# Two-bank projection tiles, wide evictions on fixed engines and a rearranged first and last step in a dilated neighbourhood-attention kernel

## The chip, the cores and the metric

The kernel runs on one core of one Trainium2 chip. The metric is device time in microseconds (us), the median of several executions; executions of one kernel mostly agree within 0.3%. Profiles are single executions and come out some 1 to 3 us shorter than the timed median, because a span runs from the first to the last instruction. The granted clock in the profiles is the share of full speed that the throttle allowed PE; it is 1.00 in the stretch of the middle shown for each kernel below, but not everywhere in the start.

Engine names in the profile: PE is the matrix engine (PEld its weight loads), DVE is VectorE, ACT is ScalarE, POOL is GpSimd, SP is SyncE, which here only issues transfers. A "q" after a name (SPq, ACTq) is that engine's sequencer, for instance issuing a transfer.

## The reference

Attention over a 7 x 7 neighbourhood with dilation 2 on a 224 x 224 image with 192 channels, one head, bfloat16.

```python
def reference(x, wqkv, wo):                       # x (1,224,224,192), wqkv (192,576), wo (192,192)
    qkv = x @ wqkv                                # q, k, v: thirds of the last axis
    r0 = clip(arange(H) - 6, 0, H - 1 - 12)       # first row and column of each window,
    c0 = clip(arange(W) - 6, 0, W - 1 - 12)       # clipped at the edges of the image
    nidx = ...                                    # 49 neighbours: r0 + 0,2..12 by c0 + 0,2..12
    logits = einsum('bnc,bnkc->bnk', q, k[nidx]) * C ** -0.5
    p = softmax(logits)
    o = einsum('bnk,bnkc->bnc', p, v[nidx]) @ wo
```

## The kernel before

Two folds make the matrix work small. Scores use `x A x` with A = Wq Wk^T times the scale (tiles `aw`), so "queries" are x times A (tiles `ga`, `gb`) and "keys" are plain copies of x in another order (`xa`, `xb`; `xb` also holds one-hot rows which meet mask rows in `gb`, so that a matmul adds the mask). The value side uses WP = Wv Wo, so `vw` = x WP is already projected; its column C is one, so the product `y` of exponentials and `vw` holds the softmax sum beside the sum itself.

The work is 28 **steps** (a row parity `rc` and a block of 16 rows `j`), each of seven **ticks**. A tick forms the scores in PSUM (`s`), takes the exponential on ScalarE (`p_sb`), multiplies it with `vw` into PSUM (`y`, one buffer), takes the reciprocal of the sum (`rs`) and writes the scaled result (`o_sb`) on VectorE, and stores it. Between ticks stand the projections of the next step: `pv` products evicted into `vw`, `pg` products evicted into the queries, `pe` products of the edge columns evicted into `ge`. The first tick of every step also makes one `oe` (48 x 192), so **`oe` on VectorE marks a step** in every trace below. The program order on each engine is the order in which the code emits.

```python
ps_go = tc.tile_pool(name="ps_go", bufs=4, space=PSUM)      # one-bank tiles for pv, pg, pe
...
def evac(out, in_, n):                                      # ScalarE or VectorE, by a running estimate
    ca, cd = 60 + 0.95 * n, 70 + 1.15 * n
    if load["A"] + ca <= load["D"] + cd: load["A"] += ca; nc.scalar.copy(out=out, in_=in_)
    else:                                load["D"] += cd; nc.vector.tensor_copy(out=out, in_=in_)
...
def make_keys(k, rc):                                       # GpSimd, reading at a step of two rows, 448 bytes
    nc.gpsimd.tensor_copy(out=oa[:, rc, cc].rearrange("p n (c r) -> p (n c) r", r=BR),
                          in_=t[:, 2 * cc, rc::2, :].rearrange("p r j -> p j r"))
...
def vw_item(k, rc, i):                                      # two key blocks: half a tile per evac
    pv = ps_go.tile([128, 2, 256], F32, name="pv", tag="go")
    ...
    for cc in range(2):
        evac(VW[h:h + 64, rc, cc, 2 * i:2 * i + 2, 0:C], pv[h:h + 64, :, 0:C], 2 * C)
...
def store(dst, src): nc.sync.dma_start(out=dst, in_=src)    # every store on SyncE
...
for ti, i in enumerate(range(NQ - 1, -1, -1)):
    T = s_stage(rc, j, i)            # scores and exponential
    ...                              # this tick's vw items
    if pend: v_stage(pend); out_stage(pend)
    ...                              # this tick's query items
    pend = T
```

The softmax here doesn't subtract the row's maximum and nothing guards it: scores larger than these inputs give would overflow.

## Time and profile before

| | us |
|---|---|
| time, median of 3 (range) | 457.87 (457.26 to 459.14) |
| `oe` of step 2 (two steps done) | 74.21 |
| `oe` of the last step, 25 steps later | 391.59 |
| span | 455.9 |

So the span divides into a start of 74.2 us, a middle of 317.4 us (12.70 us a step) and an end of 64.3 us. These are the marks, from VectorE's timeline (start, duration, engine, line, operation, out<-in with shapes, count; in brackets the idle time before it and what ended it):

```profile
74.21 0.35 DVE L436 TENSOR_TENSOR oe<-y,rse 48x192 bf16<-48x192 f32 x1
...
391.59 0.35 DVE L436 TENSOR_TENSOR oe<-y,rse 48x192 bf16<-48x192 f32 x1
```

The middle, as a stretch from 110 to 136 us: its length, then busy time (and instructions) of PE, PEld, DVE, ACT and POOL, the granted clock, the DMA share and GB/s. PE and VectorE are at 81%, nothing is full.

```profile
110.00:136.00 26.00, 21.04 (x529) 18.71 (x525) 21.10 (x53) 18.84 (x41) 16.60 (x25) 1.00 0.49 112
```

Groups of instructions (line, engine, operation, shapes, count; busy us, mean ns of one; idle time before them and what ended most of it). Both engines empty halves of `pv` in small pieces; ScalarE waits 36.8 us in all for VectorE's half of the same tile, and PE's `y` waits for the outputs (54.3 us):

```profile
L231 DVE CAST vw<-pv 64x384 bf16<-64x384 f32 x237 | 130.6, 554 | 45.3 <-PE pv L259 26.4
L411 PE MATMUL y<-vw,p_sb 128*64 128x193 bf16 (+1 forms) x1540 | 102.6, 248 | 59.8 <-DVE o_sb L452 54.3
...
L228 ACT CAST vw<-pv 64x384 bf16<-64x384 f32 x169 | 79.5, 472 | 42.2 <-DVE vw L231 36.8
```

The end, from SyncE's timeline: the last output is formed at 401 us, and from 405.2 on SyncE issues 72 stores in 48.75 us, 0.68 us each.

```profile
385.67 7.58 SPq L416 DMA_DIRECT2D out_dram<-o_sb  x7
393.35 11.75 SPq L416 DMA_DIRECT2D out_dram<-oe  x16
405.20 48.75 SPq L416 DMA_DIRECT2D out_dram<-o_sb  x72
```

### The profile page before, as it was taken

Reading aid. Unit: us, or ns where it says so; the run is one execution under the profiler, and the core shown is the slowest. Engines: PE = TensorE matmul, PEld = TensorE weight load, DVE = VectorE, ACT = ScalarE, POOL = GpSimd, SP = SyncE. Lnnn points to the kernel's source line nnn. Section 1 sums busy time; section 2 is a strip of 40 time slices with the busy share of each in tenths; the row PEclk is TensorE's granted clock in tenths of the full one; section 3 lists DMA queues with packets and bytes.
Section 4 is the critical chain, followed back from the end, with each engine's and each line's share of the span. In section 5 each row is a group of like instructions: output and inputs, shape, how many; then the busy total and the mean of one; then the engine's idle time right before and its main releaser. Section 6 shows DMA issues by size and latency. Waiting matters only on the chain.

```text
span 455.9 us, 17843 instructions
## 1 busy us (share of the span) xinstructions
PE 311.7 (68%) x7448; PEld 272.8 (60%) x7448; DVE 313.4 (69%) x764; ACT 281.8 (62%) x592; POOL 244.2 (54%) x393
## 2 busy tenths in 40 slices
PE   4734588788887988797878988787878887600000
PEld 2434478787777877786767877777767777500000
DVE  6586688887887877887787877887788887610000
ACT  6423677787777777787777777787776877400000
POOL 8999981776749292947658193857658200000000
PEclk9977999999999999999999999999999999955555
DMA  9316536364362636373472838273452222100000
GB/s 204 85 23 142 133 121 152 91 140 107 76 145 73 150 85 155 78 140 94 97 139 56 149 78 163 71 151 91 96 135 62 64 54 63 36 9 20 20 8 4
DMA packets 108607, 42.85 MB, mean 94 GB/s; under 512 B 83204, under 2 KB 108270, under 8 KB 108526
## 3 DMA queue, kind: packets, MB, share of 16 engines
q1 hardware_dynamic: 108078, 41.42, 40.4%
q8 instruction: 58, 0.95, 1.0%
q10 hardware_dynamic: 448, 0.30, 0.3%
q14 instruction: 23, 0.19, 0.1%
HBM read 0.29 MB, written 19.35 MB: 43 GB/s over the span
## 4 chain that ended last, share of the span: by engine, by line
DVE 31%; PE 28%; ACT 11%; issue 8%; DMA 5%; POOL 4%; SPq 1%; DVEq 0%; ACTq 0%; POOLq 0%
DVE vw L231 12%; DVE o_sb L452 11%; PE y L411 10%; PE pg L321 6%; PE pv L259 5%; DMA out_dram<-o_sb 5%; ACT vw L228 4%; DVE rs L450 4%; PE s_88 L392 3%; ACT p_sb L395 3%; PE s_87 L392 2%; PE pe L279 1%; ACT ga_100 L228 1%; ACT gb_104 L228 1%; POOL xb_93 L240 1%
## 5 line engine op out<-in xcount | busy, mean ns | idle before, releaser
L231 DVE CAST vw<-pv 64x384 bf16<-64x384 f32 x237 | 130.6, 554 | 45.3 <-PE pv L259 26.4
L411 PE MATMUL y<-vw,p_sb 128*64 128x193 bf16 (+1 forms) x1540 | 102.6, 248 | 59.8 <-DVE o_sb L452 54.3
L411 PEld LDWEIGHTS <-p_sb 128*64 128x64 bf16 (+1 forms) x1540 | 78.3, 106 | 78.9 <-issue 75.8
L452 DVE TENSOR_TENSOR o_sb<-y,rs 128x384 bf16<-128x384 f32 x196 | 109.3, 558 | 7.0 <-DVE rs L450 0.3
L228 ACT CAST vw<-pv 64x384 bf16<-64x384 f32 x169 | 79.5, 472 | 42.2 <-DVE vw L231 36.8
L321 PEld LDWEIGHTS <-aw 128*64 128x64 bf16 x1008 | 61.8, 112 | 2.2 <-issue 1.1
L395 ACT ACTIVATE p_sb<-s_87 128x448 bf16<-128x448 f32 x98 | 53.5, 546 | 10.5 <-PE s_87 L392 9.3
L395 ACT ACTIVATE p_sb<-s_88 128x448 bf16<-128x448 f32 x98 | 53.5, 546 | 8.0 <-PE s_88 L392 6.2
L392 PEld LDWEIGHTS <-xa_90 128*64 128x64 bf16 x532 | 48.8, 111 | 2.2 <-issue 0.6
L392 PEld LDWEIGHTS <-xa_91 128*64 128x64 bf16 x532 | 49.1, 110 | 1.5
L392 PEld LDWEIGHTS <-xb_93 128*64 128x64 bf16 x420 | 36.8, 112 | 19.9 <-issue 16.4
L392 PEld LDWEIGHTS <-xa_92 128*64 128x64 bf16 x448 | 41.1, 110 | 1.3
L450 DVE RECIPROCAL rs<-y 128x2 f32<-128x2 f32 x196 | 32.2, 164 | 13.6 <-PE y L411 11.0
L228 ACT CAST ga_100<-pg 128x436 bf16<-128x436 f32 x55 | 28.5, 521 | 19.2 <-PE pg L321 18.7
L228 ACT CAST ga_101<-pg 128x436 bf16<-128x436 f32 x51 | 26.5, 522 | 19.7 <-PE pg L321 19.5
L392 PEld LDWEIGHTS <-xb_94 128*64 128x64 bf16 x420 | 37.3, 111 | 1.0
L259 PE MATMUL pv<-WP,xa_90 128*64 128x192 bf16 x280 | 32.1, 254 | 0.8 <-POOL xa_90 L238 0.6
L392 PEld LDWEIGHTS <-xb_95 128*64 128x64 bf16 x336 | 28.8, 111 | 3.3 <-DVE gb_104 L231 1.2
L392 PEld LDWEIGHTS <-xb_96 128*64 128x64 bf16 x336 | 29.5, 111 | 2.1 <-issue 1.0
L259 PE MATMUL pv<-WP,xa_91 128*64 128x192 bf16 x280 | 30.7, 246 | 0.0
L259 PE MATMUL pv<-WP,xb_93 128*64 128x192 bf16 x224 | 25.7, 255 | 1.5 <-POOL xb_93 L240 1.5
L259 PE MATMUL pv<-WP,xa_92 128*64 128x192 bf16 x224 | 24.8, 246 | 0.0
(226 smaller groups left out, 1068.9 us busy)
## 6 DMA issues: line engine op xcount, KB each, us to landing
out_dram<-o_sb SPq DMA_DIRECT2D x162, 96.0 KB
out_dram<-o_sb SPq DMA_DIRECT2D x27, 60.0 KB
out_dram<-oe SPq DMA_DIRECT2D x54, 9.0 KB
out_dram<-o_sb SPq DMA_DIRECT2D x54, 12.0 KB
out_dram<-o_sb SPq DMA_DIRECT2D x54, 9.0 KB
xb_95<-xb_93 SPq DMA_DIRECT2D x4, 112.0 KB
xb_96<-xb_94 SPq DMA_DIRECT2D x4, 112.0 KB
xe_97<-xa_90 SPq DMA_DIRECT2D x1, 448.0 KB
```

The source lines that it names most:

```text
L228: nc.scalar.copy(out=out, in_=in_)
L231: nc.vector.tensor_copy(out=out, in_=in_)
L240: nc.gpsimd.tensor_copy(out=ob[ps, rc, cc].rearrange("p n (c r) -> p (n c) r", r=BR), in_=t[ps, 1, rc::2, :].rearrange("p r j -> p j r"))
L259: nc.tensor.matmul(pv[h:h + 64, m, 0:C], lhsT=keys(k, rc, cc)[kt][:, 2 * i + m, :], rhs=WP[:, cc, kt, :], start=(kt == 0), stop=(kt == 1))
L279: nc.tensor.matmul(pg[64 * h:64 * h + 64, g], lhsT=AW[w][:, 64 * h:64 * h + 64], rhs=r, start=(i == 0), stop=(i == 1))
L321: nc.tensor.matmul(pg[64 * h:64 * h + 64, a_ - ra:b_ - ra, :], lhsT=AW[w][:, 64 * h:64 * h + 64], rhs=xt[b][:, k, l, :], start=(i == 0), s ...
L392: nc.tensor.matmul(o[h:h + 64, :, rs], lhsT=keys(k, rc, cc)[kt][:, n, :], rhs=mv[:, cc, CW * n:CW * n + QW, rs], start=(kt == 0), stop=(kt ...
L395: nc.scalar.activation(out=T.p[:].rearrange("p a b -> p (a b)"), in_=ps[:, 0:4 * QW * BR], func=ACTF.Exp)
L411: nc.tensor.matmul(o, lhsT=l, rhs=rhs, start=st, stop=True, skip_group_check=True)
L450: nc.vector.reciprocal(out=rs[:], in_=y_bank[:, :, sl, C:C + 1])
L452: nc.vector.tensor_tensor(out=o[:], in0=y_bank[:, :, sl, 0:C], in1=rs[:].to_broadcast([128, 2, C]), op=ALU.mult)
```

## The change

The intent: fewer and wider evictions, less work for GpSimd, an earlier start and an end that isn't a queue of store issues.

- Projection tiles take two PSUM banks (two slots instead of four). A `pv` tile holds four key blocks; VectorE evicts one half of the partitions in one 64 x 768 copy, ScalarE the other. Queries are evicted by ScalarE in 128 x 848 copies; the high half goes to a staging tile `hs` that GpSimd splits.
- Keys are copied in an order that GpSimd can read at unit stride.
- In a tick, `y` and the output come ahead of the projections.
- Outputs of two tiles at the end of a step are scaled in one instruction; small stores go to GpSimd's queue. In the last step outputs are gathered in `oall` and stored by few transfers on three queues.
- At the start, masks and one-hots are partly spread by transfers, the first keys are shared by VectorE and GpSimd, and work that the first scores don't need is deferred into steps 0 and 1.

```diff
-    ps_go = ctx.enter_context(tc.tile_pool(name="ps_go", bufs=4, space=PSUM))
+    ps_go = ctx.enter_context(tc.tile_pool(name="ps_go", bufs=2, space=PSUM))
 ...
+    mask_cols(4, nc.vector.tensor_copy); mask_rows(4, 0, nc.vector.tensor_copy)
 ...
+    for k in range(2):
+        nc.vector.memset(s_bank[k][:], NEG)
     for cc in range(2):
         h = 64 * ((1 + cc) % 2)
-        nc.gpsimd.memset(VW[h:h + 64, 0, cc, :, 0:C], 0.0)
+        nc.vector.memset(VW[h:h + 64, 0, cc], 0.0)
 ...
-            nc.gpsimd.tensor_copy(out=oa[:, rc, cc].rearrange("p n (c r) -> p (n c) r", r=BR),
-                                  in_=t[:, 2 * cc, rc::2, :].rearrange("p r j -> p j r"))
+        eng(out=dst.rearrange("p n (r c) -> p r n c", c=CW),
+            in_=t[ps, 2 * cc if kt == 0 else 1, rc::2, :].rearrange("p r (n c) -> p r n c", c=CW))
 ...
-            pv = ps_go.tile([128, 2, 256], F32, name="pv", tag="go")
+            pv = ps_go.tile([128, 2, 2, 256], F32, name="pv", tag="go")
-            for cc in range(2):
-                evac(VW[h:h + 64, rc, cc, 2 * i:2 * i + 2, 0:C], pv[h:h + 64, :, 0:C], 2 * C)
+            for cc, eng in ((0, nc.vector.tensor_copy), (1, nc.scalar.copy)):
+                eng(out=VW[h:h + 64, rc, cc, n0:n1, 0:C], in_=pv[h:h + 64]...[:, 0:n1 - n0, 0:C])
 ...
+            if kind < 2:
+                put(nc.scalar.copy, A[:, kind], slice(0, 128))
+            elif direct: ...
+            else:
+                hs = work.tile([128, SQ, BR], BF, name="hs", tag="hs", bufs=2)
+                put(nc.scalar.copy, hs[:], slice(0, 128))
+                for cc in range(2): nc.gpsimd.tensor_copy(out=Bt[ps, cc, 6:S, ra:rb], in_=hs[ps, 6:S, ra:rb])
 ...
+    last_qs = [nc.sync, nc.gpsimd, nc.scalar]
+        def pick(q):
+            if not last: return q
+            qn[0] += 1
+            return last_qs[qn[0] % 3]
 ...
-            for _ in range(-(-len(v_q) // left)): v_q.pop(0)()
             if pend:
                 v_stage(pend)
                 out_stage(pend)
+            for _ in range((len(v_q) > (NQ - ti) // 2) + (len(v_q) > NQ - ti)): v_q.pop(0)()
```

## The prediction

> **What bounds it now.** Three stages with different limits. (1) Start: by the timeline the second score tick runs at 39.8 us; VectorE builds masks from 25.6 to 37.6 us in front of evacuations, and GpSimd copies eight key tiles (1.70 us each) before the edge columns. (2) Middle: the `oe` instruction, one per step, goes from 62.3 to 379.9 us in 25 steps, 12.7 us each. By busy time over 110 to 136 us PE has 81%, VectorE 81%, ScalarE 72%, GpSimd 64%: none is full; the chain of waits (DVE 31%, PE 28%) runs y, reciprocal, `o_sb`, y with `vw` evacuations between. (3) End: the last `o_sb` is done at 401 us, the span is 455.9. Store issues fill it: 72 `o_sb` stores from 405.2 take SP 48.75 us, 0.68 us each.
>
> **What changes, costed.**
> - End: after the last output about 24 stores remain, 8 on each of three queues: 6 us at 0.7 us, 2 us landing, more on GpSimd: about 9 us. Saves 45 us.
> - Start: masks by DMA, first keys shared by VectorE and GpSimd, all else later. First score tick at 18-19 us; but steps 0 and 1 take deferred work, so 14 and 16 us. `oe` of step 2 at about 50 us, now 74.2: saves about 23 us.
> - Middle, per step: 14 `vw` halves (0.554 us VectorE, 0.472 ScalarE) become 4 + 4; a 64x768 one should take 0.95 and 0.79 us (slopes from narrower ones). Eight query evacuations become three of 128x848, 0.88 us. VectorE falls to 8.9 us, ScalarE stays at 9.3, PE about 10.2 (twice the edge matmuls). GpSimd's key copies get unit-stride reads; the Trainium skill, GPSIMD Engine Reference, Performance pitfalls for Q7 kernels, puts reads at steps over 8 bytes about 50% dearer; here the 224-byte-step copy takes 1.72 us, one as long with a small step 0.92. So 4 x about 1 us plus two `hs` copies and two DMA issues, under 10 us.
>
> **Why I do not book the busy time saved.** In the changed program's order ScalarE's `vw` evacuation waits for VectorE's of the same tile (serialized now too: 36.8 us of "ACT vw <- DVE vw"), and the next exponential stands behind it. The chain over two ticks, `o_sb`, vw on VectorE 0.95, vw on ScalarE 0.79, exp 0.55, y 0.53, reciprocal and o 0.77, is about 3.5 us; three pairs and the single tick with its double output give 12.4 to 13 us a step. Wider evacuations lengthen this latency while the sum shrinks. So the middle stays near 12.7 us.
>
> **Sum.** 50 + 25 x 12.7 + 11 (last step) + 9 = 388, plus 2 us between span and time: **390 us**, range **368 to 405**. Faster by over 2%: 0.98; within: 0.015; slower: 0.005.
>
> **What would show it.** Right: last `o_sb` to end of span under 12 us; `oe` of step 2 near 50 us; 12.2 to 13.2 us per step; "ACT vw <- DVE vw" among the longest waits; key copies near 1 us; PE still about 80% busy in the middle. Wrong: a step of 11 us or less, set by PE, would mean the vw chain overlaps better (about 345 us in all); key copies still 1.7 us with GpSimd over 90% busy would mean 13 us or more from GpSimd; a tail over 15 us would mean stores on GpSimd or ScalarE cost more than 0.7 us.

(The "224-byte-step copy" is a slip: the code reads every second row of 112 bfloat16 values, a step of 224 elements or 448 bytes.)

## The result, and the profile after

The changed kernel takes **418.7 us** (418.11 to 418.88). Ratios here are the mean time of one kernel's fast runs over that of the other's of the same rounds, so not quite the ratio of the medians quoted: 0.9137, interval 0.9103 to 0.9171. It is faster by 8.6%, and 28.7 us slower than predicted; the predicted range (368 to 405) does not hold it.

The same marks as above divide the span of 417.1 us:

```profile
74.18 0.35 DVE L462 TENSOR_TENSOR oe<-y,rse 48x192 bf16<-48x192 f32 x1
...
393.54 0.35 DVE L462 TENSOR_TENSOR oe<-y,rse 48x192 bf16<-48x192 f32 x1
```

| part | before | predicted | after |
|---|---|---|---|
| start, to `oe` of step 2 | 74.21 | 50 | 74.18 |
| middle, per step | 12.70 | 12.7 | 12.77 |
| end, from the last `oe` | 64.3 | 20 | 23.6 |

All of the gain comes from the end (40.7 us); the middle gives 2 us back, and the start gives nothing.

**The middle.** In the same stretch of 26 us VectorE fell from 21.1 to 17.7 us of work and ScalarE from 18.8 to 17.5, and the step did not shorten:

```profile
110.00:136.00 26.00, 22.48 (x563) 20.48 (x559) 17.71 (x39) 17.46 (x30) 16.05 (x32) 1.00 0.46 109
```

The wide evictions cost what was predicted (64 x 768: 0.95 us on VectorE, 0.79 on ScalarE; the means below mix in 64 x 384). The wait in front of ScalarE's has more than tripled, and `y` now waits for the exponential:

```profile
L271 ACT CAST vw<-pv 64x768 bf16<-64x768 f32 x116 | 82.7, 713 | 122.9 <-DVE vw L271 122.8
L425 PE MATMUL y<-vw,p_sb 128*48 128x193 bf16 (+1 forms) x1540 | 103.2, 251 | 53.5 <-ACT p_sb L413 43.1
...
L271 DVE CAST vw<-pv 64x768 bf16<-64x768 f32 x116 | 98.5, 850 | 7.3 <-PE pv L267 5.4
```

How these two belong together is seen by laying three timelines of one tick side by side. First VectorE's: it evicts its half of a `pv` tile, until 154.24.

```profile
153.28 0.96 DVE L271 CAST vw<-pv 64x768 bf16<-64x768 f32 x1
```

ScalarE's timeline: the other half starts 0.03 us after that, and only then comes the exponential of scores `s_88`, which PE had finished at about 153.45.

```profile
154.27 0.79 ACT L271 CAST vw<-pv 64x768 bf16<-64x768 f32 x1 [1.10 <-DVE vw L271]
154.97 0.54 ACT L413 ACTIVATE p_sb<-s_88 128x448 bf16<-128x448 f32 x1
```

PE's timeline: `y` follows the exponential.

```profile
155.56 0.52 PE L425 MATMUL y<-vw,p_sb 128*64 128x193 bf16 x8 [0.63 <-ACT p_sb L413]
```

The exponential waited 1.5 us with its input ready, and PE 0.63 us for it. (The chain of waits puts this stretch down mostly to PE, since PE had just finished the next scores, `s_87`, when the exponential began. The order of instructions on ScalarE tells otherwise: the exponential stands behind `vw`.)

**The start.** VectorE fills the score banks and `vw` from 18.4 to 22.8 us in front of the edge eviction `ge`, for which PE (3.8 us) and GpSimd (9.7 us) wait; then it builds row one-hots and row masks (4.5 us) behind a `vw` eviction of the first tick. VectorE's timeline:

```profile
18.44 0.48 DVE L229 MEMSET s_87<- 128x512 f32 x1
18.98 0.48 DVE L229 MEMSET s_88<- 128x512 f32 x1
19.74 1.19 DVE L233 MEMSET vw<- 64x1358 uint32 x1 [0.28 <-issue]
21.27 1.19 DVE L233 MEMSET vw<- 64x1358 uint32 x1 [0.34 <-issue]
...
23.18 0.38 DVE L243 COPY xb_93<-xt_81 64x896 bf16<-64x896 bf16 x1
23.60 0.46 DVE L298 CAST ge<-pe 128x288 bf16<-128x288 f32 x1
...
27.79 0.95 DVE L271 CAST vw<-pv 64x768 bf16<-64x768 f32 x1 [2.65 <-PE pv L267]
28.77 2.42 DVE L164 COPY xb_94<-t_r 32x896 bf16<-32x896 bf16 x2
31.20 2.08 DVE L148 COPY gb_104<-rm 32x944 bf16<-32x944 bf16 x2
```

The list of waits (who waited for whom: us in all, times, longest) names both who wait:

```profile
POOL ga_100 L316 <- DVE ge L298: 9.7, 1, 9.7
...
PE pg L339 <- DVE ge L298: 6.2, 8, 3.8
```

The first exponential comes at 29.6 us (before: 31.6), step 0 takes 22.9 us and step 1 16.5.

Step 0 has one more thing in it. The granted clock is 0.50 from about 33.7 to 40.3 us, after PE had done almost nothing since 31.4 us, and 0.88 over the step. The step as a window (columns as above):

```profile
34.73:57.65 22.92, 16.20 (x299) 14.42 (x300) 14.41 (x27) 12.82 (x21) 10.49 (x24) 0.88 0.44 107
```

The version called base below does the same PE work in step 0 at a clock of 1.00, with 13.7 us of busy PE in 19.9 us. So a part of the 22.9 us may be a slower PE and not waiting. No run here sets the clock, and none tests whether the pause before it brings the drop on, so the part stays open.

**The end.** After the last output (406.2 us) 11 us remain, near the predicted 9. But the last step itself takes 12.6 us from `oe` to the last output. ScalarE's timeline shows three store issues, 3.1 us, in front of an exponential:

```profile
393.41 0.54 ACT L413 ACTIVATE p_sb<-s_87 128x448 bf16<-128x448 f32 x1
393.92 3.11 ACTq L442 DMA_DIRECT2D out_dram<-oe  x3
397.13 0.54 ACT L413 ACTIVATE p_sb<-s_88 128x448 bf16<-128x448 f32 x1 [3.18 <-DMA out_dram<-oe]
```

GpSimd's key copies take 0.93 us instead of 1.72, as expected. The Trainium skill, GPSIMD Engine Reference, section "Performance pitfalls for Q7 kernels", puts reads at a step over 8 bytes at about +50%; the trace agrees in direction and shows more, a factor of 1.85 (the write pattern changed with it). GpSimd is busy for 64% of the middle before and 62% after, so I expect no time from this by itself; no run tests it.

### The profile page after: what moved, and what is told of

It is laid out like the page before. It is cut to its first block, busy times and chain, and to the rows that moved or that the text cites. A ratio compares the mean times of both kernels' runs of the same rounds, so it can differ in the third digit from the quotient of the medians.

```text
span 417.1 us, 17787 instructions
## 1 busy us (share of the span) xinstructions
PE 320.7 (77%) x7616; PEld 289.5 (69%) x7616; DVE 268.2 (64%) x572; ACT 246.9 (59%) x417; POOL 240.4 (58%) x511
## 4 chain that ended last, share of the span: by engine, by line
PE 56%; DVE 22%; ACT 12%; issue 4%; DMA 2%; ACTq 1%; POOL 1%; POOLq 0%; DVEq 0%
PE y L425 19%; PE pg L339 15%; DVE o_sb L475 10%; PE pv L267 9%; ACT p_sb L413 8%; PE s_88 L410 5%; PE s_87 L410 5%; DVE vw L271 5%; DVE rs L470 3%; ACT vw L271 2%; PE pe L295 2%; DMA w_hi<-in_wqkv_dram 1%; DVE ge L298 1%; DVE oall L475 1%; POOL out_dram L442 1%
## 5 line engine op out<-in xcount | busy, mean ns | idle before, releaser
L271 ACT CAST vw<-pv 64x768 bf16<-64x768 f32 x116 | 82.7, 713 | 122.9 <-DVE vw L271 122.8
L425 PE MATMUL y<-vw,p_sb 128*48 128x193 bf16 (+1 forms) x1540 | 103.2, 251 | 53.5 <-ACT p_sb L413 43.1
L425 PEld LDWEIGHTS <-p_sb 128*48 128x48 bf16 (+1 forms) x1540 | 68.5, 106 | 64.0 <-ACT p_sb L413 52.3
L271 DVE CAST vw<-pv 64x768 bf16<-64x768 f32 x116 | 98.5, 850 | 7.3 <-PE pv L267 5.4
L440 POOL DMA_DIRECT2D out_dram<-o_sb x27 | 15.6, 578 | 124.0 <-DVE o_sb L475 124.0
L339 PEld LDWEIGHTS <-aw 128*64 128x64 bf16 x1008 | 52.5, 112 | 16.8 <-issue 14.4
L410 PEld LDWEIGHTS <-xa_91 128*64 128x64 bf16 x532 | 51.6, 112 | 1.6
L410 PEld LDWEIGHTS <-xa_90 128*64 128x64 bf16 x532 | 50.8, 112 | 1.5
L410 PEld LDWEIGHTS <-xa_92 128*64 128x64 bf16 x448 | 43.2, 111 | 1.3
L410 PEld LDWEIGHTS <-xb_93 128*64 128x64 bf16 x420 | 37.4, 112 | 5.4 <-issue 4.3
L410 PEld LDWEIGHTS <-xb_94 128*64 128x64 bf16 x420 | 38.4, 112 | 1.0
L410 PEld LDWEIGHTS <-xb_96 128*64 128x64 bf16 x336 | 30.5, 111 | 1.0
L410 PEld LDWEIGHTS <-xb_95 128*64 128x64 bf16 x336 | 30.4, 111 | 0.8
L267 PE MATMUL pv<-WP,xa_90 128*64 128x192 bf16 x280 | 27.8, 251 | 3.7 <-DVE ge L298 3.3
L267 PE MATMUL pv<-WP,xa_91 128*64 128x192 bf16 x280 | 27.1, 247 | 1.7 <-ACT vw L271 1.7
L345 ACT CAST ga_100<-pg 128x848 bf16<-128x848 f32 x28 | 24.0, 857 | 5.1 <-PE pg L339 5.1
L345 ACT CAST hs<-pg 128x848 bf16<-128x848 f32 x26 | 22.4, 861 | 3.1 <-PE pg L339 2.1
L267 PE MATMUL pv<-WP,xb_93 128*64 128x192 bf16 x224 | 22.5, 252 | 0.0
```

The lines of the kernel that those rows point to most:

```text
L267: nc.tensor.matmul(pv[h:h + 64, (n - n0) // 2, (n - n0) % 2, 0:C], lhsT=keys(k, rc, cc, kt)[:, n, :], rhs=WP[:, cc, kt, :], start=(kt == 0 ...
L271: eng(out=VW[h:h + 64, rc, cc, n0:n1, 0:C], in_=pv[h:h + 64].rearrange("p a b c -> p (a b) c")[:, 0:n1 - n0, 0:C])
L339: nc.tensor.matmul(pr[64 * h:64 * h + 64, g, a_ - 4 * g:b_ - 4 * g, :], lhsT=AW[w][:, 64 * h:64 * h + 64], rhs=xt[b][:, k, l, :], start=(i ...
L345: eng(out=dst[:, 6:S].rearrange("p s (g r) -> p s g r", r=4), in_=src)
L410: nc.tensor.matmul(o[h:h + 64, :, rs], lhsT=keys(k, rc, cc, kt)[:, n, :], rhs=(A, Bt)[kt][:, cc, CW * n:CW * n + QW, rs], start=(kt == 0), ...
L425: nc.tensor.matmul(o, lhsT=l, rhs=rhs, start=st, stop=True, skip_group_check=True)
```

## The experiments

Eighteen kernels were run, in five groups, each on one chip beside the kernel before, whose median in the groups was 457.2 to 458.0. They ran three to five rounds. The groups ran on four chips, so a difference of under 1 us between two groups is not resolved. "Base" below means the 374.7 us version of the first group.

| run | built on | us, median (range) | ratio to before | `oe` of step 2 | us per step, 2 to 27 |
|---|---|---|---|---|---|
| (changed kernel) | | 418.7 | 0.9137 | 74.18 | 12.77 |
| m_exp | changed kernel | 383.77 (382.29 to 384.05) | 0.8378 | 74.21 | 11.39 |
| b_tail | kernel before | 415.20 (414.76 to 415.42) | 0.9069 | 74.03 | 12.69 |
| s_all | changed kernel | 409.75 (409.50 to 410.02) | 0.8952 | 65.35 | 12.75 |
| all ("base") | s_all with m_exp | 374.72 (374.65 to 374.84) | 0.8187 | 65.35 | 11.35 |
| s_fill | changed kernel | 415.39 (415.34 to 416.93) | 0.9074 | 70.31 | |
| s_rows | changed kernel | 415.27 (413.67 to 415.88) | 0.9056 | 69.00 | |
| s_ownq | changed kernel | 417.25 (416.07 to 418.12) | 0.9104 | 71.03 | |
| s_tr | changed kernel | 417.92 (416.65 to 418.42) | 0.9117 | 72.30 | |
| t_late | changed kernel | 415.25 (414.56 to 416.10) | 0.9071 | 73.28 | 12.77 |
| s_order | base | 374.58 (373.97 to 376.14) | 0.8187 | 66.66 | |
| s_exp01 | base | 376.82 (376.10 to 377.57) | 0.8231 | 67.71 | |
| best | s_order, s_exp01, t_late | 373.33 (372.42 to 373.84) | 0.8158 | 67.24 | |
| s_split | base | 373.83 (373.26 to 374.24) | 0.8167 | 64.95 | |
| s_edge | base | 372.06 (370.74 to 375.01) | 0.8138 | 62.59 | |
| s_mask | base | 375.47 (375.08 to 375.61) | 0.8202 | 64.53 | |
| best2 | s_split, s_edge, s_mask, t_late | 368.12 (367.50 to 368.49) | 0.8046 | 60.63 | |
| s_more | base | 381.43 (380.52 to 382.41) | 0.8319 | 70.93 | |
| best3 | s_split, s_edge, t_late | **367.67** (367.46 to 368.86) | 0.8030 | 61.98 | 11.35 |

One caution for the column of `oe`: the weights' second part (`w_hi`) lands between 5.1 and 7.3 us in these profiles, for every kernel alike, so the start of a single profile can shift for that reason alone. Three profiles share one start: in the changed kernel, m_exp and t_late it lands at 7.33, 6.13 and 5.99 us, the first score matmul comes at 28.0, 27.1 and 27.0 us, and `oe` of step 2 at 74.18, 74.21 and 73.28. The granted clock in step 0 differs too: 0.83 to 0.92 in the runs built on the changed kernel (1.00 in s_all), 1.00 in those built on the base except s_exp01 (0.92) and best (0.84). Medians of time are the safer measure.

### Where the middle's saving went: m_exp

Theory: the exponential stands behind ScalarE's `vw` eviction, which waits for VectorE's. Rival: PE, at 86%, sets the step. A build that defers the eviction in every step locks up (a `pv` tile keeps its slot while the next is asked for), so it was deferred from step 2 on only.

```diff
-            for cc, eng in ((0, nc.vector.tensor_copy), (1, nc.scalar.copy)):
-                ...
+            put(0, nc.vector.tensor_copy)
+            owed.append(lambda: put(1, nc.scalar.copy))     # given out later ...
+            if not late[0]:                                 # ... from step 2 on
+                settle()
 ...
             T = s_stage(rc, j, i)                           # scores and exponential
+            settle()                                        # ... behind the next exponential
```

> The changed kernel with one order changed from step 2 on: ScalarE's evacuation of a vw tile is put after the next tick's exponential, not before it. Chain theory: a pair of ticks is held by o_sb, vw on VectorE, vw on ScalarE, exp, y, o_sb (3.64 us measured); with the exponential ahead the pair falls to what PE needs (about 3.1 us), a step from 12.77 to about 11.2 us, the whole to about 380 us (372 to 390), and waits of y for the exponential (43 us) nearly vanish. Rival: PE's own work holds the middle (the chain that ended last puts 56% of the span on PE); then a step stays within 0.3 us of 12.77 and the whole at 412 to 420 us.

Measured: 383.77 us, so 34.9 us less than the changed kernel. No instruction was added or taken away; one kind of them moved. The step fell from 12.77 to 11.39 us, PE rose from 22.5 to 24.4 of 26 us, and the wait of ScalarE's eviction from 122.8 to 29.5 us. The wait of `y` for the exponential fell from 43.1 to 3.7 us. The stretch from 110 to 136 us in m_exp:

```profile
110.00:136.00 26.00, 24.35 (x611) 21.93 (x608) 19.00 (x42) 20.14 (x32) 18.45 (x36) 1.00 0.56 114
```

And from its list of waits:

```profile
ACT vw L271 <- DVE vw L271: 29.5, 49, 4.3
...
PE y L435 <- ACT p_sb L423: 3.7, 2, 2.6
```

The order on ScalarE in the trace is now exponential, then eviction, and the eviction finds VectorE's already done or nearly:

```profile
155.66 0.54 ACT L423 ACTIVATE p_sb<-s 128x448 bf16<-128x448 f32 x1
156.42 0.55 ACT L423 ACTIVATE p_sb<-s 128x448 bf16<-128x448 f32 x1 [0.22 <-PE s L420]
157.15 0.79 ACT L271 CAST vw<-pv 64x768 bf16<-64x768 f32 x1 [0.19 <-DVE vw L271]
```

So PE was not the limit at 12.77, but it is close to one at 11.39 (94% busy). The saving in engine time that the change brought was hidden behind the order on ScalarE, and one reordered line releases 1.4 us a step. What isn't shown is how much of the 11.39 us needs the wide evictions: the same reordering was not tried on the kernel before, where PE and VectorE are each busy for 10.3 of the 12.7 us of a step.

On the serialization itself: the two evictions of a tile read disjoint halves of the partitions. The Trainium skill, PSUM — Partial Sum Buffer, section "PSUM bank collisions raise a hardware error", says that two engines may not be in one bank and one 32-partition quadrant at once, but that different quadrants of one bank may be used at the same time. By that page the two could run together. In the built program a semaphore makes ScalarE wait for VectorE, and in the changed kernel's trace ScalarE's eviction waited for VectorE's 114 times out of 116. No run takes that wait away, so what overlapping them would gain stays open.

### How much is the end alone: b_tail

The kernel before, with only the last step's output part taken from the change (`oall`, few transfers, three queues).

```diff
     def out_stage(T):
-        ...                                   # every store on SyncE
+        (out_last if T.j == NJ else out_before)(T)   # out_last: the changed kernel's last step
```

> The kernel before with one part of the change alone: the last step's stores (about 40, on three queues, in place of 96 on one). From the oe instruction of the last step to the end of the span the kernel before takes 64.3 us and the changed one 23.6, so if the whole gain of the change is this part, this run takes 457.9 - 40.7 = 417 us (414 to 420), and oe of step 2 and the 12.7 us per step stay as they were. The rival, that the start and the middle gained something on their own, expects 422 us or more here.

Measured: 415.2 us, 42.6 us less than before in the same rounds, and **3.5 us better than the whole change**. The rest of the change, taken together and as it stands, costs time.

### The last exponentials behind store issues: t_late

```diff
             qn[0] += 1
-            return last_qs[qn[0] % 3]
+            return last_qs[qn[0] % (3 if i < 2 else 2)]   # ScalarE's queue only once no exponential is left
```

> The changed kernel (418.7 us) with one edit: the last step's stores go to ScalarE's queue only from the point where no exponential is left, before that to SyncE's and GpSimd's alone. In the changed kernel three oe stores (3.1 us) and two oall stores (1.5 us) stand in front of exponentials of the last step, and the last output comes 12.6 us after the last oe. Theory 'store issues on ScalarE hold the last exponentials': last oe to last output 9.5 to 10.5 us, the tail after it 11 us as before, the whole at 416 to 417. Rival 'the last step is set by something else (y, VectorE)': 418.4 to 419.

Measured: 415.25 us, 3.4 less than the changed kernel; the median lies a little under the expected 416 to 417. The last `oe` to the last output is 9.4 us instead of 12.6, and the rest to the end 11.1 us as before. The exponentials now follow their scores:

```profile
392.46 0.98 ACT L413 ACTIVATE p_sb<-s 128x448 bf16<-128x448 f32 x2
394.03 0.55 ACT L413 ACTIVATE p_sb<-s 128x448 bf16<-128x448 f32 x1 [0.59 <-PE s L410]
395.40 0.54 ACT L413 ACTIVATE p_sb<-s 128x448 bf16<-128x448 f32 x1 [0.82 <-PE s L410]
```

### The start, four repairs: s_all, s_fill, s_rows, s_ownq, s_tr, and all

The four edits, alone and together:

```diff
 s_fill:  -    nc.vector.memset(VW[...]) (6 fills, ahead of the first edge eviction)
          +    nc.gpsimd.memset(VW[...])  (behind GpSimd's two key copies, where it was idle)
 s_rows:  -    onehot_rows(1, nc.vector.tensor_copy); mask_rows(1, 2, nc.vector.tensor_copy)   (in the first tick)
          +    onehot_rows(1, nc.scalar.copy);        mask_rows(1, 2, nc.scalar.copy)          (ahead of the first queries)
 s_ownq:  -    return 2 if (rc, j) == (1, NJ) else rc                  # steps 0 and 1 share a query buffer
          +    return 2 if (rc, j) in ((0, 0), (1, NJ)) else rc
 s_tr:    both transposes of a tile ahead of its two copies
```

> The changed kernel with four repairs of the start: the vw memsets on GpSimd where it idles (14.4 to 24.1 us), the first step's own query buffer, the row masks and row one-hots of step 1 on ScalarE before the first scores, and the weight transposes of a tile issued before its copies. If the four waits lie one behind another on the start's critical path, their sum is 3.4 + 3.4 + 4 + 1.2 = 12 us: 407 us, oe of step 2 at 62 us in place of 74.2. Rival: they run beside other work that ends as late (GpSimd's eight key copies from 25.8 to 34 us and the edge copies behind them, or the vw chain of the extra tiles of step 0), and less than 5 us comes back: 414 us or more.

> One repair alone: the memsets of vw go from VectorE, where they stand in front of the first edge evacuation (18.4 to 23.6 us), to GpSimd, which idles from 14.4 to 24.1 us. On the critical path: ge starts at about 20.2 us, the first exponential 3.4 us earlier at about 26 us, and the whole 3.4 us shorter, 415.3 us. If something else ends as late, the first exponential moves but oe of step 2 and the whole stay within 1 us.

> One repair alone: row one-hots and row masks of step 1 leave VectorE, where they run from 28.8 to 33.3 us between two vw evacuations, for ScalarE, idle from 16.1 to 20.3 us. On the critical path: oe of step 0 at about 30.5 us in place of 34.7 and the whole 4 us shorter, 414.7 us. Rival: GpSimd's key and edge copies (to 35.8 us) end as late and less than 1.5 us comes back.

> One repair alone: the first step gets its own query buffer (it shares one with step 1, so its score matmuls wait for evacuations of step 1's queries: 1.85 + 1.59 + 0.29 us). On the critical path: 3.4 us shorter, 415.3 us. If the waits only hide the vw chain behind them, within 1 us of 418.7.

> One repair alone: the weight transposes of one tile are all issued before its two copies, so PE does not wait 0.41 us for the first copy three times. At most 1.2 us shorter: 417.5 us; if the memsets on VectorE then hold the start, within 0.5 us of 418.7.

Together 9.0 us (409.75), alone 3.3, 3.4, 1.5 and 0.8, the same sum; the last two are too small to be told from nothing by their intervals. The theory behind them holds in kind: VectorE's fills and masks did stand in front of the first ticks. But the size is short of what was expected of them together (407, with `oe` of step 2 at 62; measured 409.75 and 65.35). The own query buffer shows better in step 0 of the profiles: 20.8 us in s_ownq against 22.3 in t_late, which has the changed kernel's start and the same granted clock in that step (0.92).

A side effect shows in s_all: GpSimd's fill of `vw` (2.36 us each) and VectorE's key copies get into each other's way. The two key copies take 2.40 and 0.52 us; the changed kernel's, with GpSimd idle, 0.79 us together. In s_all, VectorE's timeline has the first of them:

```profile
17.07 2.40 DVE L238 COPY xb<-xt 64x896 bf16<-64x896 bf16 x1
```

and GpSimd's the two fills, until 19.2 us:

```profile
14.45 4.76 POOL L496 MEMSET vw<- 64x2716 bf16 x2
```

The Trainium skill, SBUF — State Buffer, section "Who interferes with whom", describes a port pair shared by VectorE and GpSimd: when VectorE copies in one of its two-port modes, one of the two holds the pair for a whole instruction while the other waits. The 2.40 us fit that (in which mode the copy ran, no view shows). ScalarE isn't part of it by that page, and the row one-hots agree: 0.93 us each on ScalarE, beside GpSimd's fill in s_all and with GpSimd idle in s_rows (the second of the two).

This wait sets a time. In every version with the fills on GpSimd and the key copies ahead of the edge eviction (s_fill, s_all, base, s_exp01, s_mask, s_more) that eviction begins at 20.0 us, though `w_hi` lands between 5.6 and 7.3 us in them: the key copies begin between 17.1 and 18.6 us and end only after GpSimd's second fill, which ends at 19.2.

About s_ownq: by the code, in the kernel before and in the changed one alike, steps 0 and 1 use one query buffer, so later ticks of step 0 would read step 1's queries. The results pass the comparison in every version, and no run here measures the difference; s_ownq removes the sharing.

> The four repairs of the start and the exponential ahead of the vw evacuation together. If start and middle are separate stages the gains add: 380 - 12 = 368 us (360 to 380).

Measured: 374.72 us, 44.0 less than the changed kernel, where the two parts alone gave 34.9 and 9.0. Start and middle are separate costs.

### The first 25 us again: s_order, s_split, s_edge

s_order put the score-bank fills first of all, formed WP in the `y` banks and put the edge product ahead of the key copies.

> This is the version with the four start repairs and ScalarE's vw eviction taken out from in front of the exponential (374.7 us, first exponential 26.9, oe of step 2 at 65.35), with only the order of the first 25 us changed: the score banks are filled at the very top while VectorE has nothing to do (2 x 0.48 us), the products WP are formed in the y banks instead of in the two-slot pool (PE waited 1.6 and 0.8 us there for aw evictions), and the edge product of block 0 is formed and evicted ahead of VectorE's key copies (2.9 us). Theory 'the start is a chain through VectorE's program order and two slots': the edge eviction ge, at 20.0 us there, comes at about 15.5 to 16.5, the first exponential at 23 to 24, oe of step 2 at 62 to 63, the whole at 371 to 373. Rival 'the rest of the start is set by the loads and by GpSimd's copies of the next keys': the first exponential moves by under 1 us and the time stays at 374 to 375.

Measured: 374.58 us, no gain. The edge eviction came at 18.8 us instead of the expected 15.5 to 16.5. The edit brought two costs of its own: with the fills at the top, VectorE's masks ended at 11.8 us instead of 9.9, and the second WP product waited for the eviction of the first, which stood behind VectorE's `aw` evictions. PE's timeline of s_order:

```profile
16.35 0.32 PE L221 MATMUL y<-wo_lo,wT_lo 128*128 128x192 bf16 x1 [5.34 <-DVE WP L224]
```

So it tested nothing cleanly, and was split up. s_split shares the `aw` evictions by tile instead of in turn:

```diff
-                if i % 2 == 0:
+                if np_ == 0:            # ScalarE takes the first tile, VectorE the second
                     nc.scalar.mul(AW[nm]...)
```

> The 374.7 us version with one edit in the start: the 16 aw evictions are shared by tile, not in turn: ScalarE takes all eight of the first product tile, VectorE all eight of the second. In the base they alternate on each tile and last from 9.25 to 13.9 us though each takes 0.22 to 0.28. Theory 'two engines on one PSUM tile take turns here as on vw': they end at about 12.0 (VectorE is only free of the masks at 9.95), the first products WP start 0.5 to 2 us earlier relative to w_hi's landing, oe of step 2 at 63.5 to 64.5, the whole at 373 to 374. Rival 'VectorE's fills and key copies behind them set the edge eviction, whenever aw ends': oe of step 2 moves by under 0.5 us and the whole stays at 374.3 to 375.

Measured: 373.83 us and `oe` of step 2 at 64.95. The `aw` evictions became shorter (from the first to the end of the last 2.7 us, where the base needs 4.2 us in turns), and WP's evictions came 1.5 us earlier after the first use of `w_hi`. Yet the edge eviction moved only from 20.03 to 19.63 us. The total, 0.9 us less, is where the theory put it, but the intervals overlap, and `oe` of step 2 moved by 0.4 us, as the rival had it. What follows on VectorE sets the edge eviction: the two key copies began 1.9 us earlier than in the base and took 3.56 us instead of 2.05, beside GpSimd's fills.

s_edge takes those away from in front of it, and nothing else:

```diff
+    q0 = q_items(0, 0, True)
+    q0.pop(0)(); q0.pop(0)()            # edge product, high-half queries
     key_copy(0, 0, 1, 1, nc.vector.tensor_copy)
     key_copy(0, 0, 0, 1, nc.vector.tensor_copy)
+    for k in range(2): nc.vector.memset(s_bank[k][:], NEG)     # was ahead of all these
```

> The 374.7 us version with the edge product of block 0 and the high-half query evictions ahead of VectorE's two key copies and the two score-bank fills (4 us of VectorE). Theory 'VectorE's program order': the edge eviction comes at about 16.7 instead of 20.0 us, the first exponential at 24 to 25 instead of 26.9, oe of step 2 at 62.5 to 63.5, the whole at 372 to 373. Rival 'loads and GpSimd': the first exponential moves by under 1 us, the whole stays at 374 to 375.

Measured: edge eviction at 16.75 us, first exponential at 24.1, `oe` of step 2 at 62.6, each where the theory put it; 372.06 us median, with one run at 375.0 that keeps the interval wide (0.8096 to 0.8180).

### Step 0 itself: s_exp01, s_mask, s_more

s_exp01 moves the exponential ahead of ScalarE's `vw` eviction in steps 0 and 1 too, settling the debt before the next `pv` tile.

```diff
             put(0, nc.vector.tensor_copy)
             owed.append(lambda: put(1, nc.scalar.copy))
-            if not late[0]: settle()
 ...
+            if not late[0]: settle()         # before the next pv tile takes a slot
             pv = ps_go.tile([128, 2, 2, 256], F32, name="pv", tag="go")
```

> The same base (374.7 us), with ScalarE's vw eviction moved behind the next tick's exponential in steps 0 and 1 as well, where there are two vw tiles in many ticks; a tile's eviction is still given out before the next vw tile takes a slot. In steps 0 and 1 of the base, oe goes 28.9, 48.8, 65.35: 19.9 and 16.5 us. Theory 'in steps 0 and 1 it is the same hold of the exponential as in the middle': step 0 becomes 17 to 18 us and step 1 14.5 to 15.5, oe of step 2 at 60 to 62, the whole at 370 to 371. Rival 'there the two slots and the sum of the extra work set the pace (the chain runs vw on VectorE, vw on ScalarE, then PE's next tile)': the exponentials come earlier, but oe of step 2 moves by under 1.5 us and the whole stays at 373.5 to 375.

Measured: 376.82 us, 2.1 slower; step 0 went from 19.9 to 21.9 us and step 1 from 16.5 to 17.3. The theory falls, and so does the rival's forecast, since `oe` of step 2 came 2.4 us later. The first exponential did come early (24.8 us). Why the steps became longer is not settled. One candidate is the granted clock. Step 0 as a window, first in the base:

```profile
28.90:48.80 19.90, 13.66 (x299) 12.02 (x295) 14.35 (x26) 11.74 (x20) 11.73 (x27) 1.00 0.44 105
```

and in s_exp01:

```profile
28.50:50.43 21.93, 15.12 (x287) 12.85 (x283) 15.12 (x27) 11.93 (x20) 12.09 (x28) 0.92 0.45 106
```

The clock is 0.50 in s_exp01 from about 44.9 to 48.2 us, and 1.5 of the 2.0 us by which step 0 grew are busy time of PE, on fewer recorded instructions (287 against 299). The other candidate is a slot that is held longer, so that PE waits for its next tile. The list of waits from 26 to 72 us doesn't bear it out. In the base:

```profile
PE pv L262 <- ACT vw L266: 3.8, 6, 1.0
PE pg L344 <- ACT vw L266: 2.9, 3, 1.6
```

and in s_exp01, where the first of these has almost gone:

```profile
PE pg L344 <- ACT vw L268: 4.5, 9, 0.7
```

Together PE waits less for these evictions, not more. One `y` does wait 1.8 us, at 42.4 us, for an eviction that was held back. So the reordering that gains 1.4 us a step in the middle loses 2 us in step 0, and no run separates what the clock and the held-back eviction contribute.

s_mask moves the row masks of later steps from step 0 into step 2.

```diff
-                mask_rows(0, 1, nc.vector.tensor_copy)    # step 0, ticks 3 and 5
-                mask_rows(5, 3, nc.vector.tensor_copy)
+            if si == 2 and ti == 1: mask_rows(0, 1, nc.vector.tensor_copy)
+            if si == 2 and ti == 4: spread_masks(2, 0, 64); mask_rows(5, 3, nc.vector.tensor_copy)
```

> The 374.7 us version with the row masks of later steps (two calls, 1.61 and 0.81 us of VectorE at 35.1 and 40.3 us, each pair between a vw eviction and a reciprocal) moved from step 0 into step 2. Theory 'they stand on step 0's chain, and step 2 has room (VectorE 73% busy there)': step 0 goes from 19.9 to 18 us, step 2 stays at 10.9 to 11.2, the whole at 372.5 to 373.5. Rival 'step 0 is set by eleven tiles through two slots, the masks only fill gaps': step 0 moves by under 0.7 us and the whole stays at 374 to 375.

Measured: step 0 0.7 us shorter, step 2 1.9 us longer (12.8 instead of 10.9), 375.47 us in all. The rival all but holds for step 0 (it had put the move at under 0.7 us), and the theory's second half, that step 2 has room, is refuted. With VectorE about 74% busy there, 1.8 us of masks in one piece held the reciprocal and the output (VectorE's timeline of s_mask):

```profile
70.48 1.79 DVE L148 COPY gb<-rm 32x944 bf16<-32x944 bf16 x2
72.31 0.17 DVE L475 RECIPROCAL rs<-y 128x2 f32<-128x2 f32 x1
72.52 0.56 DVE L480 TENSOR_TENSOR o_sb<-y,rs 128x384 bf16<-128x384 f32 x1
```

and, since there is one `y` buffer, PE (its timeline):

```profile
73.13 0.52 PE L430 MATMUL y<-vw,p_sb 128*64 128x193 bf16 x8 [1.82 <-DVE o_sb L480]
```

s_more doubles a part of what is left: step 0 forms three of its seven `vw` tiles twice, to the same place.

```diff
-            v_q = v0 + v_q
+            again = v_units(jn, rn)
+            v_q = v0 + v_q[:1] + again[:1] + v_q[1:2] + again[1:2] + v_q[2:3] + again[2:3] + v_q[3:]
```

> The 374.7 us version, where step 0 forms three of its seven vw tiles twice, right after each other (the same values into the same place, so the result is right). Theory 'step 0 is paced by tiles through two slots, each held for its matmuls (0.86 us) and two evictions in turn (0.96 and 0.80 us), so 1.3 us a tile at best': step 0 goes from 19.9 to 24 to 25.5 us, and the whole to 379 to 380.5. Rival 'PE's own work paces it' (13.7 of the 19.9 us busy): only the matmuls add, 2.6 us or less, so under 22.5 us and under 377.5. Rival 'the tiles have room, the chain from y to reciprocal to o paces it': under 1.5 us more.

Measured: step 0 24.1 us instead of 19.9, in the range of the slot theory and over both rivals' limits (22.5 and 21.4 us); 381.43 us in all, 6.7 more, a little over the expected. The granted clock is 1.00 in step 0 of both. The price of a tile is higher than the theory's 1.3 us at best: by VectorE's timeline only two of the three added tiles lie between the marks of step 0 (ten against eight), and the third comes before the first `oe` and delays it by 1.4 us. Up to the `oe` of step 2 three tiles cost 5.6 us, 1.86 us each. So two slots emptied in turn are a part of the price and not all of it. The wait of ScalarE's evictions for VectorE's grows with the tiles. The list of waits within step 0 of the base:

```profile
ACT vw L266 <- DVE vw L266: 7.8, 6, 2.2
```

and of s_more:

```profile
ACT vw L266 <- DVE vw L266: 10.7, 8, 2.2
```

### The versions: best, best2, best3

> All of it together: the four start repairs, the exponential ahead of ScalarE's vw eviction in every step, the changed order of the first 25 us, and no store on ScalarE while an exponential is left. If the gains add as those before did (s_all 9.0 and m_exp 34.9 gave 44.0 together): 374.7 less about 2.5 for the order, less 0 to 4 for steps 0 and 1, less 2 for the last stores, so 366 to 370 us. If they share a cause (the last step of this version is faster than the changed kernel's, so that its stores hold less), 370 to 372.

> The 374.7 us version with these three edits and the store edit of t_late, which was worth 3.4 us on the changed kernel. If all four theories hold and the gains add: 374.7 less 1, 2, 1.7 and 3.4, so 366 to 368 us; if the three rivals hold, 370.5 to 372.

> The 368.1 us version without the mask move, which made step 2 longer by 1.9 us and step 0 shorter by 0.7: 367 us (366.3 to 367.7).

best (with s_order and s_exp01, both of which proved useless or worse) gave 373.33, against 370 to 372 in the less favourable of its two cases. best2 gave 368.12, between its two sums. best3, without the mask move, gave 367.67, inside the expected range; the two overlap, so the mask move's cost isn't resolved between them. best3 beats both kernels: 0.803 of the kernel before, interval 0.8011 to 0.8050. In its middle PE is busy 24.09 of 26 us.

## Why the prediction was right or wrong

**Right: faster by over 2%.** It was given 0.98. The end alone brought it; b_tail, with nothing but that part, is 3.5 us faster.

**Right: the middle.** "So the middle stays near 12.7 us": 12.77 measured. The reason held too, and m_exp shows it: moving one instruction out of the way takes the step to 11.39 us, near the 11 us at which the prediction had put a step set by PE. PE's own work was sized a little short: 10.2 us a step predicted, 11.0 busy in the changed kernel. The estimates of the wide evictions (0.95 and 0.79 us) and of the query eviction (0.88; measured 0.86) were right.

**Nearly right: the end.** "11 (last step) + 9" was 20; measured 23.6. Of the missing 3.6 us t_late accounts for 3.2: store issues on ScalarE stand in front of the last exponentials. The prediction named the third queue but didn't ask what else is in that queue.

**Wrong: the start.** The step that failed is "First score tick at 18-19 us; but steps 0 and 1 take deferred work, so 14 and 16 us. `oe` of step 2 at about 50 us, now 74.2: saves about 23 us." Measured 74.18: it saves nothing. This term alone is 24.2 of the 28.7 us by which the total missed; the end is 3.6, the middle 1.9 (1 us more than the total, from rounding and from the 2 us allowed between span and time). By its terms:

| term | predicted | changed kernel | best3 |
|---|---|---|---|
| first score matmul | 18.5 | 28.0 | 21.2 |
| from there to the first `oe` | about 1.5 | 6.7 | 4.1 |
| step 0 | 14 | 22.9 | 20.1 |
| step 1 | 16 | 16.5 | 16.6 |
| `oe` of step 2 | 50 | 74.2 | 62.0 |

What the runs showed in its place:

- The prediction shows no working for the first two terms. The runs show that they go through VectorE's program order: fills, key copies, one-hots and masks in front of the edge eviction and the first `vw` evictions (s_fill, s_rows and s_edge, 3.3, 3.4 and 2.7 us of time). Work was taken off GpSimd, which then stood idle for 9.7 us, and put on the engine that everything waited for.
- Step 0 at 14 us is a common step of 12.7 us plus 1.3 us for its deferred work; that 1.3 us is what was mis-sized. Between the marks step 0 holds eight `vw` tiles, where a common step holds four (half-width ones counted). At the 1.86 us a tile of s_more, four more tiles are 7.4 us (an estimate from that run), which is as much as the base's step 0 (19.9 us) lies above the 12.7. But step 1 holds seven tiles and lies only 3.8 us above it, 1.3 us for each of three more, so the count of tiles is not the whole account. At that lower price four tiles are 5 us.
- Step 0 of the changed kernel is 3 us longer still than the base's. At least two things are in that difference, and their shares are open: the query buffer that steps 0 and 1 share (1.6 us between s_ownq and t_late), and the granted clock of 0.88 (PE is busy for 2.5 us more than in the base). The prediction asked about neither. The masks in step 0 are worth 0.7 us at most (s_mask).
- Step 1 was right.

Not settled: best3's start is still 12 us over the prediction: 2.7 us to the first score, 2.6 us from there to the first `oe`, 6.1 us of step 0 and 0.6 us of step 1. The estimate of 5 to 7.4 us for the tiles, in place of 1.3, covers 3.7 us or all of step 0's part; nothing here covers the first two. In best3's profile the granted clock is 0.50 from about 19.9 to 23.3 us, which covers the first score, and no run shows what that costs.

## What to carry to other kernels

A saving in busy time becomes a saving in time only if the chain that closes each round gets shorter: look up, engine by engine in program order, what the next critical instruction stands behind, and move the uncritical one back; but see first whether the moved one holds a buffer that the next round needs (moved in every step, this one locked up). When two engines empty one tile in turn, a wider tile lengthens the chain while it shrinks the sum (here 0.55 + 0.47 us a tile became 0.95 + 0.79, for half as many tiles). And a start or an end must be costed by the order of instructions on the busiest engine, not by when its inputs land; "the engine is idle a quarter of the time" doesn't mean that a piece of work fits in. Look at the granted clock of each stage before a longer stage is put down to waits.

## What the Trainium skill lacked or had wrong

- GPSIMD Engine Reference, "Performance pitfalls for Q7 kernels": a read at steps over 8 bytes is given about +50%. The key copy, the same elements at a 448-byte step instead of unit steps, took 1.72 us against 0.93, +85%. (The write pattern changed with it; no run separates the two.)
- PSUM — Partial Sum Buffer, "PSUM bank collisions raise a hardware error": it allows two engines in different quadrants of one bank, and its rule calls guarding by whole banks the simple version, but it doesn't say that a program may be given such a wait, or what it costs. Here that wait is 122.8 us of ScalarE's time in the changed kernel, and 16 `aw` evictions that two engines took in turns on each tile lasted 4.2 us, against 2.7 us when each engine had a tile of its own (s_split).
- SBUF — State Buffer, "Who interferes with whom": nothing wrong; what it lacks is a figure for this case: a VectorE key copy of about 0.4 us took 2.40 us beside a GpSimd fill of 2.36 us.
- DMA: Bandwidth & Descriptors, "Latency and other measured facts" and "SWDGE vs HWDGE vs iDMA": they give first-byte latencies (about 0.6 us by hardware, about 1 us from GpSimd) and call the hardware route the faster to set up. For the set-up the skill has rough parts only: about 50 ns of sequencer dispatch and a small, variable descriptor generation on this page, and "a few hundred ns" on the SBUF page. I found no figure for how long an issue holds the issuing engine's own stream. It was 0.68 us on SyncE, 1.04 us for the three on ScalarE that held an exponential, and 0.58 us on GpSimd.
